# Hedgehog attention, a two-dimensional Fourier mix and an FFN on one core: a loop of batches against one woven order

## The chip, the cores and the metric

One core of a Trainium2 chip. The time is device microseconds of one execution; the table below gives the median of three runs of the kernel before.

## What is computed

For each of 8 batches, 8 heads, 576 positions and 64 channels per head, the attention maps queries and keys through 128 features and both signs, then mixes without a softmax; the result of all heads, 576 x 512 numbers, goes through a Fourier mix, a layer norm and an FFN with a hidden width of 2,048.

```python
def phi(x):
    proj = einsum('bhsd,df->bhsf', x, w_phi)
    proj = proj - max(abs(proj), axis=-1)
    return concatenate([exp(proj), exp(-proj)], axis=-1)
kv = einsum('bhsf,bhsd->bhfd', phi(k), v); z = sum(phi(k), axis=2)
x = (phi(q) @ kv) / (phi(q) @ z + 1e-06)          # heads side by side: 576 x 512
u = x + real(fft(fft(x, axis=1), axis=2))
un = (u - mean(u)) / sqrt(var(u) + 1e-06)          # per row
out = u + maximum(un @ w_ch1, 0) @ w_ch2
```

Inputs and outputs are float32; the kernels compute their matmuls in bf16.

## The kernel before

A batch goes through three functions. `attention_stage` loads queries, keys and values with 15 DMAs on POOL's queue, 128 positions each, which turn float32 to bf16 on the way, and turns queries and keys with ten DMA transposes on SP (L195, L196) into QT and KT, which have one buffer each. `attention_core` loops over the 8 heads. For each it projects the queries twice, once with features on the partitions (psqh, L210 and L214, for the exponentials QPhp and QPhn) and once with positions on the partitions (psqs, L225, only for the largest absolute value), and the keys once (pskk, L235). VectorE takes the maxima (L243, L246), ScalarE the exponentials (L220, L221, L260, L261), VectorE scales the values (L264, L268); then come the key-value products (L276), the products with the queries (psnum, L290 and L296), and the division on VectorE (L306 to L313) into X. 64 contraction rows per projection means half of the array's rows.

`fft_ffn` copies X to bf16 (XB, L325), takes column means with a matmul of ones (pmb) and column sums (pcs), and subtracts the means (XF). The DFT over positions is 80 matmuls of 288 columns (psD, L361; in every group of five the last has 64 rows); the one over channels is 40 of 512 columns (psu, L385 and L390). U is their sum with X. Row statistics are taken with VectorE, an inverse square root by shifts and Newton steps on small tiles (L416 to L443), the scaled rows on ScalarE (UN, L449), and TensorE transposes them (pUT, L456). The FFN is 128 matmuls of 288 columns with a relu on ScalarE per group of four (psh, L474 and L481) and 80 of 512 columns (pso, L486), whose sum with U is stored.

The cosine and sine tables are made at the start by `gen_dft` with VectorE and ScalarE, 36 sines over blocks of 288 or 256 columns. The two FFN weights load once. The outer loop stages batch b + 1, runs its `attention_core`, and then `fft_ffn` of batch b; a scheduler orders the instructions by what they depend on, with the DFT's front end at a high priority.

Of the kernel before, what the change touches and what calls it, by code (L numbers as in the profile page):

```python
# [10 lines left out]
AT = mybir.ActivationFunctionType  # L12
# [3 lines left out]
F32R = mybir.dt.float32r  # L16
BF16 = mybir.dt.bfloat16
I32 = mybir.dt.int32

BATCH_LIST = None  # L20
DEBUG_DUMP = False

MAGIC = 12582912.0


@with_exitstack
def kernel(
# [15 lines left out]
    NSC = 5  # L43
    NCC = C // 128
    NHH = HID // 128
    assert (B, H, S, D, DF, C, HID) == (8, 8, 576, 64, 128, 512, 2048)

    def msz(js):
        return 128 if js < 4 else 64

    batches = list(range(B)) if BATCH_LIST is None else list(BATCH_LIST)

    const = ctx.enter_context(tc.tile_pool(name="const", bufs=1))
    stage = ctx.enter_context(tc.tile_pool(name="stage", bufs=2))
    transp = ctx.enter_context(tc.tile_pool(name="transp", bufs=1))
    headp = ctx.enter_context(tc.tile_pool(name="headp", bufs=2))
    small = ctx.enter_context(tc.tile_pool(name="small", bufs=4))
    dwork = ctx.enter_context(tc.tile_pool(name="dwork", bufs=2))
    xpool = ctx.enter_context(tc.tile_pool(name="xpool", bufs=2))
    fpool = ctx.enter_context(tc.tile_pool(name="fpool", bufs=1))  # L60
    outp = ctx.enter_context(tc.tile_pool(name="outp", bufs=2))
    psumA = ctx.enter_context(tc.tile_pool(name="psumA", bufs=2, space=bass.MemoryType.PSUM))
    _psumB = [None]

    def get_psumB():
        if _psumB[0] is None:
            _psumB[0] = ctx.enter_context(tc.tile_pool(name="psumB", bufs=4, space=bass.MemoryType.PSUM))
        return _psumB[0]
# [3 lines left out]
    eps_ap = const.tile([128, 1], F32, name="eps_ap")  # L72
    nc.vector.memset(eps_ap[:], 1e-06)
    sc2 = const.tile([128, 2, NSC], F32, name="sc2")
    nc.vector.memset(sc2[:, 0, :], 2.0)
    nc.vector.memset(sc2[:, 1, :], -1.0)

    wphi2 = const.tile([128, DF], BF16, name="wphi2")
    nc.gpsimd.dma_start(out=wphi2[0:64, :], in_=w_phi[:, :])
    nc.gpsimd.dma_start(out=wphi2[64:128, :], in_=w_phi[:, :])  # L80

    W1b = const.tile([128, NCC, HID], BF16, name="W1b")
    W2b = const.tile([128, NHH, 512], BF16, name="W2b")

    _wloaded = []

    def load_ffn_weights():
        if _wloaded:
            return
        _wloaded.append(True)  # L90
# [3 lines left out]
    onesS_b = const.tile([128, 128], BF16, name="onesS_b")  # L94
    nc.vector.memset(onesS_b[:], 1.0 / S)
    ones2_b = const.tile([128, 2], BF16, name="ones2_b")
    nc.vector.memset(ones2_b[:], 1.0)
    ident_b = const.tile([128, 128], BF16, name="ident_b")
    make_identity(nc, ident_b[:])

    CS_r = const.tile([128, NSC, S], BF16, name="CS_r")
    SS_r = const.tile([128, NSC, S], BF16, name="SS_r")
    CD_r = const.tile([128, NCC, C], BF16, name="CD_r")
    SDn_r = const.tile([128, NCC, C], BF16, name="SDn_r")

    def gen_dft(gen, dst_cos, dst_sin, nchunks, N, sin_sign, rowk, pcol):
        half = N // 2
        last = None
        for j in range(nchunks):
            for hb in range(2):  # L110
                mm = gen.tile([128, half], F32, tag="mm", name="mm")
                nc.vector.tensor_scalar_mul(
                    out=mm[:], in0=rowk[:, half * hb: half * hb + half], scalar1=pcol[:, j: j + 1]
                )
                q1 = gen.tile([128, half], F32, tag="q1", name="q1")
                nc.vector.tensor_single_scalar(out=q1[:], in_=mm[:], scalar=1.0 / N, op=ALU.mult)
                kq = gen.tile([128, half], F32, tag="kq", name="kq")
                nc.vector.tensor_scalar(
                    out=kq[:], in0=q1[:], scalar1=MAGIC, scalar2=MAGIC,
                    op0=ALU.add, op1=ALU.subtract,  # L120
                )
                mr = gen.tile([128, half], F32, tag="mr", name="mr")
                nc.vector.scalar_tensor_tensor(
                    out=mr[:], in0=kq[:], scalar=-float(N), in1=mm[:],
                    op0=ALU.mult, op1=ALU.add,
                )
                last = nc.scalar.activation(
                    out=dst_sin[:, j, half * hb: half * hb + half], in_=mr[:],
                    func=AT.Sin, scale=sin_sign * 2.0 * np.pi / N * (1.0 - 1e-7),
                )  # L130
                kqc = gen.tile([128, half], F32, tag="kqc", name="kqc")
                nc.vector.tensor_scalar(
                    out=kqc[:], in0=q1[:], scalar1=0.25, scalar2=MAGIC,
                    op0=ALU.add, op1=ALU.add,
                )
                kqc2 = gen.tile([128, half], F32, tag="kqc2", name="kqc2")
                nc.vector.tensor_single_scalar(
                    out=kqc2[:], in_=kqc[:], scalar=MAGIC, op=ALU.subtract
                )
                mrc = gen.tile([128, half], F32, tag="mrc", name="mrc")  # L140
                nc.vector.scalar_tensor_tensor(
                    out=mrc[:], in0=kqc2[:], scalar=-float(N), in1=mm[:],
                    op0=ALU.mult, op1=ALU.add,
                )
                last = nc.scalar.activation(
                    out=dst_cos[:, j, half * hb: half * hb + half], in_=mrc[:],
                    func=AT.Sin, scale=2.0 * np.pi / N * (1.0 - 1e-7), bias=halfpi[:],
                )
        return last

    def generate_constants():
        with tc.tile_pool(name="genc", bufs=1) as genc, tc.tile_pool(
            name="gent", bufs=1
        ) as gen:
            rowk_i = genc.tile([128, 640], I32, name="rowk_i")
            nc.gpsimd.iota(rowk_i[:], pattern=[[1, 640]], base=0, channel_multiplier=0)
            rowk = rowk_i[:].bitcast(F32)
            nc.vector.tensor_copy(out=rowk, in_=rowk_i[:])
            pcol_i = genc.tile([128, 9], I32, name="pcol_i")
            nc.gpsimd.iota(pcol_i[:], pattern=[[128, 9]], base=0, channel_multiplier=1)  # L160
            pcol = pcol_i[:].bitcast(F32)
            nc.vector.tensor_copy(out=pcol, in_=pcol_i[:])
            gen_dft(gen, CS_r, SS_r, NSC, S, 1.0, rowk, pcol)
            last = gen_dft(gen, CD_r, SDn_r, NCC, C, -1.0, rowk, pcol)
        return last

    def attention_stage(b):
        QS = stage.tile([128, NSC, H * D], BF16, tag="QS", name="QS")
        KS = stage.tile([128, NSC, H * D], BF16, tag="KS", name="KS")
        VS = stage.tile([128, NSC, H, D + 1], BF16, tag="VS", name="VS")  # L170
        nc.vector.memset(QS[64:128, NSC - 1, :], 0.0)
        nc.vector.memset(KS[64:128, NSC - 1, :], 0.0)
        nc.gpsimd.memset(VS[64:128, NSC - 1, :, :], 0.0)  # L173
        nc.vector.memset(VS[:, 0:NSC - 1, :, D:D + 1], 1.0)
        nc.vector.memset(VS[0:64, NSC - 1, :, D:D + 1], 1.0)
        for j in range(NSC):
            rows = msz(j)
            s0 = 128 * j
            nc.gpsimd.dma_start(
                out=QS[0:rows, j, :].rearrange("p (h d) -> p h d", h=H),  # L180
                in_=q[b, :, s0:s0 + rows, :].rearrange("h p d -> p h d"),
            )
            nc.gpsimd.dma_start(
                out=KS[0:rows, j, :].rearrange("p (h d) -> p h d", h=H),
                in_=k[b, :, s0:s0 + rows, :].rearrange("h p d -> p h d"),
            )
            nc.gpsimd.dma_start(
                out=VS[0:rows, j, :, 0:D],
                in_=v[b, :, s0:s0 + rows, :].rearrange("h p d -> p h d"),
            )  # L190
        QT = transp.tile([128, H // 2, 128 * NSC], BF16, tag="QT", name="QT")
        KT = transp.tile([128, H // 2, 128 * NSC], BF16, tag="KT", name="KT")
        for j in range(NSC):
            s0 = 128 * j
            nc.sync.dma_start_transpose(out=QT[:, :, s0:s0 + 128], in_=QS[:, j, :])  # L195
            nc.sync.dma_start_transpose(out=KT[:, :, s0:s0 + 128], in_=KS[:, j, :])  # L196

        return (QS, KS, VS, QT, KT)

# [347 lines left out]
```

## Time and profile before

| | before |
|---|---|
| median of 3 runs | 892.1 us (885.8 to 893.01) |
| profiled execution, its span | 893.2 us |
| TensorE, weight loads, VectorE, ScalarE, GpSimd busy | 673.9, 391.1, 467.0, 420.9, 110.2 us |
| mean granted TensorE clock | 0.893 |
| bytes read and written in HBM | 36.77 and 9.44 MB |

The profile is one execution. A busy share of TensorE counts its pipelined matmuls from start to modelled end, so a full slice says that work was there, not that it went at the highest rate. The granted clock is given as a share of 2.4 GHz; 0.5 is 1.2 GHz.

### The profile page before, as it was taken

What the parts mean: (1) busy time and instruction counts of PE and PEld (TensorE: products, weight loads), DVE (VectorE), ACT (ScalarE), POOL (GpSimd) and SP (SyncE); (2) the same over time, 40 slices, a digit from 0 to 9 for tenths busy, and PEclk for the clock granted to TensorE, in tenths of its full rate; (3) what the DMA queues carried; (4) which work ended last, traced back from release to release, by engine and by line L of the source; (5) the groups of instructions that cost most, each with busy time, mean ns of one, the idle gap of its engine ahead of it and who ended that gap; (6) DMA issues with size and microseconds to landing.
All of it is one profiled execution on the core that took longest, in us unless ns stands there. A gap on an engine that the chain in (4) does not pass through costs nothing.

```text
span 893.2 us, 13139 instructions
## 1 busy us (share of the span) xinstructions
PE 673.9 (75%) x5000; PEld 391.1 (44%) x5032; DVE 467.0 (52%) x1366; ACT 420.9 (47%) x886; POOL 110.2 (12%) x140
## 2 busy tenths in 40 slices
PE   0112439795996699795996699787996799699887
PEld 0002324463454445363454445364544545364463
DVE  8575635851477316951477316960577237833411
ACT  2599434373255425373155425373256606470270
POOL 8710140014000320014000320010000000000000
PEclk9999999877996889877996889878996899689989
DMA  9992190029100980029100980019100310001001
GB/s 99 147 196 19 32 107 1 1 30 110 54 1 1 93 82 18 1 27 113 54 2 1 90 85 18 1 26 73 43 1 1 59 54 1 1 1 48 6 1 53
DMA packets 164094, 39.15 MB, mean 44 GB/s; under 512 B 156864, under 2 KB 158912, under 8 KB 164032
## 3 DMA queue, kind: packets, MB, share of 16 engines
q0 software_dynamic: 115264, 18.39, 31.2%
q1 hardware_dynamic: 48768, 19.94, 10.9%
q8 instruction: 39, 0.64, 0.3%
q14 instruction: 23, 0.19, 0.1%
HBM read 36.77 MB, written 9.44 MB: 52 GB/s over the span
## 4 chain that ended last, share of the span: by engine, by line
PE 64%; ACT 11%; DVE 8%; DMA 6%; SPq 6%; issue 2%; POOL 2%; DVEq 0%; ACTq 0%; POOLq 0%
PE pso L486 16%; PE psh L474 12%; PE psD L361 12%; PE psu L385 4%; PE psu L390 3%; DMA VS<-in_v_dram 3%; SPq L195 3%; PE pskk L276 3%; SPq L196 3%; DMA QT<-QS 3%; PE pskk L235 3%; PE psqs L225 2%; PE psqh L210 2%; DVE MM L246 2%; PE psnum L290 2%
## 5 line engine op out<-in xcount | busy, mean ns | idle before, releaser
L474 PE MATMUL psh<-UNT,W1b 128*128 128x288 bf16 x1024 | 161.8, 320 | 16.7 <-ACT HT L481 16.7
L486 PE MATMUL pso<-W2b,HT 128*128 128x512 bf16 (+1 forms) x624 | 140.8, 380 | 0.8
L474 PEld LDWEIGHTS <-W1b 128*128 128x128 bf16 x1024 | 107.4, 109 | 57.9 <-issue 19.7
L481 ACT ACTIVATE HT<-psh 128x288 bf16<-128x288 f32 x256 | 97.9, 415 | 52.2 <-PE psh L474 46.0
L491 DVE TENSOR_TENSOR OUT<-pso,U 128x512 f32<-128x512 f32 (+1 forms) x40 | 27.6, 690 | 169.7 <-PE pso L486 169.7
L368 ACT CAST DT<-psD 128x288 bf16<-128x288 f32 x64 | 24.9, 404 | 155.2 <-PE psD L361 154.9
L486 PEld LDWEIGHTS <-HT 128*128 128x128 bf16 (+1 forms) x640 | 63.5, 100 | 73.5 <-issue 3.4
L276 PE MATMUL pskk<-VSCp,KPp 128*128 128x65 bf16 x320 | 23.4, 210 | 73.1 <-DVE VSCp L264 50.7
L361 PEld LDWEIGHTS <-XF 128*128 128x128 bf16 (+1 forms) x640 | 52.5, 98 | 55.3 <-issue 29.8
L243 DVE TENSOR_REDUCE MM<-psqs 128x5 f32<-128x640 f32 x64 | 52.7, 824 | 38.9 <-PE psqs L225 37.3
L220 ACT ACTIVATE QPhp<-psqh 128x640 bf16<-128x640 f32 x64 | 45.0, 704 | 53.3 <-PE psqh L214 48.5
L260 ACT ACTIVATE KPp<-pskk 128x640 bf16<-128x640 f32 x64 | 45.0, 702 | 52.2 <-DVE MM L246 39.0
L235 PE MATMUL pskk<-wphi,KT 64*128 64x128 bf16 x320 | 36.1, 248 | 39.8 <-DMA KT<-KS 38.1
L361 PE MATMUL psD<-CS_r,XF 128*128 128x288 bf16 (+1 forms) x320 | 62.8, 299 | 0.0
L361 PE MATMUL psD<-SS_r,XF 128*128 128x288 bf16 (+1 forms) x320 | 60.9, 298 | 0.0
L210 PE MATMUL psqh<-QT,wphi 64*128 64x512 bf16 x64 | 31.0, 484 | 39.4 <-DMA QT<-QS 29.7
L225 PE MATMUL psqs<-wphi,QT 64*128 64x128 bf16 x320 | 37.0, 258 | 25.8 <-ACT QPhn L221 21.1
L306 DVE TENSOR_TENSOR tmpg<-psnum,EE 128x325 f32<-128x325 f32 x64 | 31.7, 495 | 47.0 <-PE psnum L296 47.0
L276 PEld LDWEIGHTS <-KPp 128*128 128x128 bf16 x320 | 18.0, 107 | 87.0 <-ACT KPn L261 48.8
L246 DVE TENSOR_REDUCE MM<-pskk 128x5 f32<-128x640 f32 x64 | 52.0, 812 | 4.1 <-PE pskk L235 2.7
L173 POOL MEMSET VS<- 64x520 bf16 x8 | 4.5, 558 | 390.0 <-DVE VSCn L268 389.9
L225 PEld LDWEIGHTS <-QT 64*128 64x128 bf16 x320 | 24.5, 112 | 53.9 <-issue 33.8
(98 smaller groups left out, 1120.8 us busy)
## 6 DMA issues: line engine op xcount, KB each, us to landing
out_dram<-OUT SPq DMA_DIRECT2D x32, 256.0 KB, 2.0
QS<-in_q_dram POOLq DMA_DIRECT2D x32, 128.0 KB, 4.8
KS<-in_k_dram POOLq DMA_DIRECT2D x32, 128.0 KB, 4.7
VS<-in_v_dram POOLq DMA_DIRECT2D x32, 128.0 KB, 5.7
W1b<-in_moe_w_ch_dram POOLq DMA_DIRECT2D x1, 2048.0 KB, 14.6
W2b<-in_moe_w_ch_dram POOLq DMA_DIRECT2D x1, 2048.0 KB, 23.8
out_dram<-OUT SPq DMA_DIRECT2D x8, 128.0 KB, 2.3
QT<-QS SPq DMA_TRANSPOSE x40, 3.8
```

Of the source, the lines that this page charges most:

```text
L210: nc.tensor.matmul(psqh[:, 0:512], lhsT=wphi2[rr, :], rhs=QT[rr, pr, 0:512], start=True, stop=True,)
L220: nc.scalar.activation(out=QPh_p[:], in_=psqh[:, 0:640], func=AT.Exp, scale=1.0)
L225: nc.tensor.matmul(psqs_v[:, jj, :], lhsT=QT[rr, pr, 128 * jj: 128 * jj + 128], rhs=wphi2[rr, :], start=True, stop=True,)
L235: nc.tensor.matmul(pskk_v[:, jj, :], lhsT=KT[rr, pr, 128 * jj: 128 * jj + 128], rhs=wphi2[rr, :], start=True, stop=True,)
L243: nc.vector.tensor_reduce(out=MM[:, 0, :], in_=psqs_v, axis=AX.X, op=ALU.max, apply_absolute_value=True)
L246: nc.vector.tensor_reduce(out=MM[:, 1, :], in_=pskk_v, axis=AX.X, op=ALU.max, apply_absolute_value=True)
L260: nc.scalar.activation(out=KPp[:], in_=pskk_v, func=AT.Exp, scale=1.0)
L276: nc.tensor.matmul(pskk[:, c0: c0 + D + 1], lhsT=KP[:, jj, :], rhs=VSC[:, jj, :], start=(jj == 0), stop=(jj == NSC - 1),)
L361: nc.tensor.matmul(psD[:, 0:288], lhsT=XF[0:M, js, 128 * cc: 128 * cc + 128], rhs=MAT[0:M, js, 288 * kb: 288 * kb + 288], start=(js == 0), ...
L474: nc.tensor.matmul(psh[:, 0:288], lhsT=W1b[:, cc, 128 * hh: 128 * hh + 128], rhs=UNT[:, cc, 288 * hf: 288 * hf + 288], start=(cc == 0), st ...
L481: nc.scalar.activation(out=out_ap, in_=psh[:, 0:288], func=AT.Relu)
L486: nc.tensor.matmul(pso[0:M, :], lhsT=HT[:, hh, 128 * kk: 128 * kk + M], rhs=W2b[:, hh, :], start=(hh == 0), stop=(hh == NHH - 1),)
```

## The change

The kernel is written anew around the same sums.

- The input is real, and only the real part of the transform is kept. The first DFT therefore works on folded channels (FEO: channel n plus or minus channel 512 - n, 256 each) and folded rows (row s plus or minus row 576 - s), with 320 table columns instead of 576, and the second one makes 320 rows; the other 256 are the same rows read backwards in channels (`pu[:, C-1:0:-1]`). So that mirrored rows stand on the same partition, queries are loaded in another order, in blocks of 16 with the exponentials' order reversed, and the output is stored in such blocks.
- Centring subtracts row 0 of X (`pm`, a matmul with one contraction row) instead of the column means.
- Projections are made for four or eight head blocks at once, in two banks, with the two halves of the contraction rows in turn; one exponential covers 1,024 columns.
- GpSimd scales the values, divides by the denominator, and folds the channels. The sum of the exponentials' scale over the values uses ScalarE for the factors.
- The factor 1/sqrt(var) is applied after the FFN, in the sum that forms the output; before it only the mean is subtracted (VectorE). GpSimd takes the power -0.5. The normalised rows are turned by DMA transposes on SP.
- 64 remaining rows of the second FFN product run on two halves of the array's columns.
- No scheduler orders the work: `weave` takes one step of a stream per letter of three strings. F is the FFN (68 steps), M attention's products and the mixing (23), T exponentials (18), P query maxima, R key maxima, S scaled values, N the norm, K, V, Q loads, A, B transposes, D row folds, W weights, C tables. A letter whose needs are not met is held and tried again. Before the first F, START has one whole batch and half of the next one's T; FIRST and PERIOD hold each step of a batch once (FIRST half of T more), PERIOD is repeated.

```diff
-        QT = transp.tile([128, H // 2, 128 * NSC], BF16, tag="QT", name="QT")
-        for j in range(NSC):
-            nc.sync.dma_start_transpose(out=QT[:, :, s0:s0 + 128], in_=QS[:, j, :])
...
+        def keys(pr):
+            psk = pj.tile([128, 2, 4, DF], F32, tag="pj", name="psk")
+            for x in range(4):
+                for jj in range(2):
+                    rr = slice(64 * jj, 64 * jj + 64)
+                    nc.tensor.matmul(
+                        psk[:, jj, x, :], lhsT=turned_k[b][0][rr, 4 * pr + x, :], rhs=wphi2[rr, :],
+                        start=True, stop=True,
+                    )
+            for sgn, KP in ((1.0, KPp), (-1.0, KPn)):
+                nc.scalar.activation(out=KP[...], in_=psk[:], func=AT.Exp, scale=sgn)
+                yield
...
+        def scale_v(pr):
+            for sgn, VC in ((1.0, VCn), (-1.0, VCp)):
+                nc.scalar.activation(out=VC[:, hs, :, D:D + 1], in_=MK[...], func=AT.Exp, scale=sgn)
+                eng = nc.vector if b == 0 and sgn < 0 else nc.gpsimd
+                eng.tensor_tensor(out=VC[:, hs, :, 0:D], in0=values[b][0][...], in1=VC[...], op=ALU.mult)
...
+        def fold(h):
+            for i, op in enumerate((ALU.add, ALU.subtract)):
+                eng = nc.vector if b == 0 and i else nc.gpsimd
+                eng.tensor_tensor(
+                    out=FEO[:, :, i, a:a + D], in0=X[:, :, a:a + D],
+                    in1=X[:, :, C - a:C - a - D:-1], op=op,
+                )
...
+            nc.gpsimd.tensor_tensor(
+                out=X[:, :, D * h:D * h + D], in0=cb[:, :, 0:D], in1=rd[:].to_broadcast([128, 5, D]), op=ALU.mult,
+            )
...
-                            psD[:, 0:288],
-                            lhsT=XF[0:M, js, 128 * cc: 128 * cc + 128],
-                            rhs=MAT[0:M, js, 288 * kb: 288 * kb + 288],
+        for i, mat, dst in ((1, SS, ET), (0, CS, DT)):
+            for mt in range(2):
+                for c in range(3):
+                    nc.tensor.matmul(
+                        ps[:, mt, 0:NK], lhsT=CEO[:, c, i, 128 * mt:128 * mt + 128],
+                        rhs=mat[:, c, :], start=(c == 0), stop=(c == 2),
+                    )
+            nc.scalar.copy(out=dst[:], in_=ps[:, :, 0:NK])
...
-                nc.scalar.activation(
-                    out=UN[0:M, kk, :], in_=U[0:M, kk, :], func=AT.Identity,
+            nc.vector.tensor_scalar(
+                out=UN[0:M, c, :], in0=X[0:M, c, 0:C], scalar1=mv[0:M, c, 0:1], op0=ALU.subtract,
+            )
+            nc.sync.dma_start_transpose(out=UT[:, :, 128 * c:128 * c + M], in_=UN[0:M, c, :])
...
+            nc.vector.scalar_tensor_tensor(
+                out=U[:, c, 0:C], in0=po[:], scalar=rs[:, c:c + 1], in1=U[:, c, 0:C],
+                op0=ALU.mult, op1=ALU.add,
+            )
+            store(b, U, c)
...
+    with tc.manual_schedule():
+        count()
+        load_first()
+        step("B")
+        step("A")
+        clear_pads()
+        weave(START + FIRST + PERIOD * (B - 1))
```

## Rows read from the trace of the kernel before

**Rows 1.** The page's busy time of each engine over the span.
```profile
PE 673.9 (75%) x5000; PEld 391.1 (44%) x5032; DVE 467.0 (52%) x1366; ACT 420.9 (47%) x886; POOL 110.2 (12%) x140
```
**Rows 2.** The page's 40 slices: busy tenths of TensorE, and its granted clock.
```profile
PE   0112439795996699795996699787996799699887
...
PEclk9999999877996889877996889878996899689989
```
**Rows 3.** The page's chain that ended last, by engine.
```profile
PE 64%; ACT 11%; DVE 8%; DMA 6%; SPq 6%; issue 2%; POOL 2%; DVEq 0%; ACTq 0%; POOLq 0%
```
**Rows 4.** The chain in order of time: start us, us, what.
```profile
185.60 4.61 PE psh L474 x22
...
319.97 10.74 PE pso L486 x49
...
420.45 10.74 PE pso L486 x49
...
871.70 10.74 PE pso L486 x49
```
**Rows 5.** Stretches of 10 us: busy us of PE, PEld, DVE, ACT, POOL; clock; DMA.
```profile
270.00:280.00 10.00, 3.50 (x32) 2.31 (x32) 9.05 (x50) 4.27 (x10) 0.00 (x0) 0.56 0.01 2
300.00:310.00 10.00, 4.01 (x29) 2.62 (x27) 0.66 (x3) 0.94 (x3) 2.54 (x4) 0.77 1.50 137
...
340.00:350.00 10.00, 10.00 (x86) 5.53 (x86) 6.45 (x19) 7.00 (x17) 0.00 (x0) 1.00 0.06 15
860.00:870.00 10.00, 10.00 (x84) 8.00 (x82) 0.00 (x0) 8.35 (x21) 0.00 (x0) 1.00 0.01 2
```
**Rows 6.** Waits (us in total, times, longest); one SP transpose of the timeline.
```profile
PE pskk L235 <- DMA KT<-KS: 38.1, 10, 17.4
...
302.39 1.35 SPq L195 DMA_TRANSPOSE QT<-QS  x1
```
**Rows 7.** Timeline of TensorE: start us, us, engine, line, operation.
```profile
17.40 0.28 PE L235 MATMUL pskk<-wphi,KT 64*128 64x128 bf16 x1 [17.40 <-DMA KT<-KS]
...
291.13 0.19 PE L290 MATMUL psnum<-kvh,QPhp 128*128 128x65 bf16 x1
...
291.41 0.19 PE L296 MATMUL psnum<-kvh,QPhn 128*128 128x65 bf16 x1
...
293.42 0.44 PE L235 MATMUL pskk<-wphi,KT 64*128 64x128 bf16 x5
...
827.45 1.71 PE L361 MATMUL psD<-CS_r,XF 128*128 128x288 bf16 x10
829.09 1.71 PE L361 MATMUL psD<-SS_r,XF 128*128 128x288 bf16 x10
```
**Rows 8.** ScalarE by line: count, then busy us, mean ns, idle before.
```profile
L481 ACT ACTIVATE HT<-psh 128x288 bf16<-128x288 f32 x256 | 97.9, 415 | 52.2 <-PE psh L474 46.0
...
L220 ACT ACTIVATE QPhp<-psqh 128x640 bf16<-128x640 f32 x64 | 45.0, 704 | 53.3 <-PE psqh L214 48.5 <-PE psnum L296 4.3 <-PE pUT L456 0.6
...
L284 ACT CAST kvh<-pskk 128x130 bf16<-128x130 f32 x64 | 17.5, 273 | 52.7 <-PE pskk L276 52.7
...
L145 ACT ACT_TABLE_LOAD x12 | 15.4, 1283 | 0.2
```
**Rows 9.** VectorE by line.
```profile
L243 DVE TENSOR_REDUCE MM<-psqs 128x5 f32<-128x640 f32 x64 | 52.7, 824 | 38.9 <-PE psqs L225 37.3
...
L306 DVE TENSOR_TENSOR tmpg<-psnum,EE 128x325 f32<-128x325 f32 x64 | 31.7, 495 | 47.0 <-PE psnum L296 47.0
...
L310 DVE RECIPROCAL rden<-comb 128x5 f32<-128x5 f32 x64 | 12.0, 187 | 1.2
```
**Rows 10.** GpSimd by line.
```profile
L179 POOL DMA_DIRECT2D QS<-in_q_dram x40 | 34.7, 869 | 82.8 <-DMA QT<-QS 43.6 <-DMA KT<-KS 30.6 <-DMA W1b<-in_moe_w_ch_dram 7.2
...
L173 POOL MEMSET VS<- 64x520 bf16 x8 | 4.5, 558 | 390.0 <-DVE VSCn L268 389.9
```
**Rows 11.** DMA issues: KB each, median us to landing.
```profile
W1b<-in_moe_w_ch_dram POOLq DMA_DIRECT2D x1, 2048.0 KB, 14.6
```

More of the change, by code (lines that the diff above doesn't have):

```diff
@@ new lines, in clear_pads, with load, make_k @@
+    def clear_pads():
+        nc.gpsimd.memset(QPHP[:, :, 576:640], 1.0)
+        nc.gpsimd.memset(QPHN[:, :, 576:640], 1.0)
+        for i in range(2):
+            nc.vector.memset(MQ[i][64:128, :, 4:5], 0.0)
+            nc.vector.memset(MV[i][64:128, 4, :], 1.0)
+    def load(pieces, which):
+        for i in which:
+            nc.gpsimd.dma_start(out=pieces[i][0], in_=pieces[i][1])
+    def make_k(b):
+        KS = stage.tile([128, H, 256], BF16, tag="KS", name="KS")
+        KS4 = stage.tile([64, H, D], BF16, tag="KS4", name="KS4")
+        pieces = [(KS4[:], k[b, :, 512:576, :].rearrange("h p d -> p h d"))]
+        for g in range(2):
+            hs = slice(4 * g, 4 * g + 4)
+            pieces.append(
+                (KS[:, hs, :], k[b, hs, 0:512, :].rearrange("h (p j) d -> p h (j d)", j=4))
+            )
+        return (KS, KS4), pieces
@@ new lines, in load_first, with turn_k @@
+    def load_first():
+        staged["k", 0], pk_ = make_k(0)
+        values[0], pv_ = make_v(0, 2)
+        staged[0], pq_ = make_q(0)
+        load(pk_, (0, 1, 2))
+        nc.gpsimd.memset(V4P[:], 0.0)
+        nc.gpsimd.memset(V4N[:], 0.0)
+        load(pv_, (2, 0, 1))
+        load(pq_, (0,))
+        load(pv_, (3,))
+        load(pq_, (1, 2, 3))
+        for name in "KVQ":
+            taken[name] = 1
+    def turn_k(KS, KS4):
+        KT = attn.tile([128, 16, 128], BF16, tag="KT", name="KT")
+        KT4 = attn.tile([128, 4, 64], BF16, tag="KT4", name="KT4")
+        nc.sync.dma_start_transpose(out=KT4[:], in_=KS4[:].rearrange("p h d -> p (h d)"))
+        for g in range(2):
+            nc.sync.dma_start_transpose(
+                out=KT[:, 8 * g:8 * g + 8, :],
+                in_=KS[:, 4 * g:4 * g + 4, :].rearrange("p h x -> p (h x)"),
+            )
+        return KT, KT4
@@ new lines, in heads @@
+        order = (4, 0, 7, 1, 6, 2, 5, 3) if b else range(H)
+        ready = {7: (0,), 6: (1,), 5: (2,), 3: (3,)} if b else {5: (3,), 6: (2,), 7: (1, 0)}
+        kvh = []
+        for h in range(H):
+            kvh.append(keyvalue(h))
+            yield
+        for h in order:
+            combine(h, kvh[h])
+            if h == 4:
+                nc.gpsimd.tensor_copy(out=X[:, :, C:C + 1], in_=X[:, :, 256:257])
+            for a in ready.get(h, ()):
+                fold(a)
+            yield
@@ new lines, in forward @@
+            store(b, U, c)
+            yield
+        po = pb.tile([128, C], F32, tag="pb", name="pso")
+        for hh in range(NHH):
+            g = 64 * (hh % 2)
+            nc.tensor.matmul(
+                po[g:g + 64, :], lhsT=HT[:, hh, 512:576], rhs=W2b[:, hh, :],
+                start=(hh < 2), stop=(hh >= NHH - 2),
+            )
+            if hh % 4 == 3 and hh < NHH - 1:
+                yield
+        for g in (0, 64):
+            nc.vector.scalar_tensor_tensor(
+                out=U[0:64, 4, 0:C], in0=po[g:g + 64, :], scalar=rs[0:64, 4:5],
+                in1=U[0:64, 4, 0:C], op0=ALU.mult, op1=ALU.add,
+            )
@@ new lines, in forward, with fetch_k, arrive_k, fetch_v @@
+        store(b, U, 4)
+        yield
+    staged, parts = {}, {}
+    def fetch_k(b):
+        staged["k", b], pieces = make_k(b)
+        load(pieces, range(3))
+        yield
+    def arrive_k(b):
+        turned_k[b] = turn_k(*staged.pop(("k", b)))
+        yield
+    def fetch_v(b):
+        values[b], pieces = make_v(b, 1)
+        load(pieces, range(3))
+        yield
+    def fetch_q(b):
+        staged[b], pieces = make_q(b)
+        load(pieces, range(4))
+        yield
+    def arrive(b):
+        turned_q[b] = turn_q(*staged.pop(b))
+        parts[b] = features(b)
+        yield
@@ new lines, in part, with run, fold_later @@
+    def part(i):
+        def run(b):
+            yield from parts[b][i]
+        return run
+    def fold_later(b):
+        yield from folds[b]
+    STREAMS = {
+        "F": (forward, 68), "M": (mixing, 23), "D": (fold_later, 2), "N": (normalise, 6),
+        "P": (part(0), 6), "T": (part(1), 18), "R": (part(2), 5), "S": (part(3), 5),
+        "K": (fetch_k, 1), "V": (fetch_v, 1), "Q": (fetch_q, 1), "A": (arrive, 1),
+        "B": (arrive_k, 1), "W": (load_ffn_weights, 2), "C": (constants, 7),
+    }
@@ new lines, in weave @@
+    def weave(plan):
+        held = []
+        for name in plan:
+            held = [x for x in held if not step(x)]
+            if name in held or not step(name):
+                held.append(name)
+        while any(taken[x] < STREAMS[x][1] * (1 if x in "WC" else B) for x in STREAMS):
+            assert any([step(x) and taken[x] < STREAMS[x][1] * B for x in STREAMS])
+    with tc.manual_schedule():
[5 more added lines that the diff above has]
+        weave(START + FIRST + PERIOD * (B - 1))
```

965 lines of the change are left out of this document (567 added, 398 removed).

## The prediction

> **What bounds the kernel now.** I read the page from the top. TensorE is busy 75% of the span, VectorE 52%, ScalarE 47%, GpSimd 12% [rows 1], so no engine is full on the whole; the slices show a first sixth with TensorE nearly empty and then a pattern that repeats [rows 2]. The chain that ended last lies 64% on TensorE, 11% on ScalarE, 8% on VectorE, 6% each on DMA and on SP's queue [rows 3]: it changes hands. The chain in order of time gives the two lengths that the sum needs [rows 4]. The first long stretch of FFN matmuls starts at 185.60; the second FFN product starts its long stretch at 319.97 for one batch and at 420.45 for the next, so a batch costs 100.5 us; the last one starts at 871.70. The profiled execution is the span of 893.2 us, 1.1 us over the median of the runs shown (892.1); I sum against 893.
>
> Inside a period, three stretches of 10 us tell why [rows 5]. At 340 TensorE is full at the full granted clock. At 270 (layer norm) VectorE is full, TensorE works 3.5 us, and the clock falls to 0.56, so to 1.2 GHz for most of it. At 300 nearly everything stands while DMA and POOL run: SP's transposes of the next batch's keys and queries have one buffer, and the key projections wait 38.1 us for KT in all, ten times [rows 6].
>
> **The prices,** at the full clock. 288 columns: 84 matmuls in 10 us, 0.119 each [rows 5]. 512 columns: 49 in 10.74, 0.219 [rows 4]. 65 columns: from 291.13 to 291.41 nine steps, 0.03 each [rows 7]. 128 columns on half the rows: five in 0.44, at most 0.088 each, and 0.04 if the 0.28 that one alone takes is its latency; I take 0.07 [rows 7]. The old DFT runs ten matmuls of 288 columns per 1.64 us, 0.165 each, where 0.119 is the price: in each group of five the last uses 64 rows, so going between whole and half array costs about 0.23 per group [rows 7]. By these a period of before holds, in us: FFN 128 x 0.119 = 15.2 and 80 x 0.219 = 17.5; DFT 80 x 0.165 = 13.2 and 40 x 0.219 = 8.8; projections 8 x 0.289 + 80 x 0.07 = 7.9; 160 small ones 4.8; means, sums and transposes 3.1. That is 70.5 of 100.5: 30 are waits and half clock.
>
> **The change, part by part.** *Folds.* Channel and row symmetry leave 12 matmuls of 320 columns for the first DFT (between 0.132, the FFN price scaled, and 0.183, the old one scaled; I take 0.15) where there were 80, 12 of 512 where there were 40, and 3 for one odd column: 1.8 + 2.6 + 0.5 = 4.9 instead of 22.0. *Centring* by an all-ones product over five chunks becomes one matmul on one row, 0.2; the column sums go; the 20 transposes on TensorE become 5 DMA transposes. *Projections* keep their 80 half-array matmuls (5.6) and 10 wide ones (8 x 0.219 + 2 x 0.11 = 2.0). *Small ones* stay: 4.8. *FFN:* 15.2, then 64 x 0.219 = 14.0 and 16 on half the columns at the same price, 3.5; two for turning the query maxima, 0.4. *Switching* between array shapes, some 12 groups beyond those in the 0.07 price, x 0.23 = 2.8. Sum: 4.9 + 0.2 + 5.6 + 2.0 + 4.8 + 15.2 + 14.0 + 3.5 + 0.4 + 2.8 = 53.4 us of TensorE per batch if half-array matmuls follow one another.
>
> They may not. The new order alternates the two halves of the rows into two banks. If pairs overlapped, the projections would fall by 3.8 and the 16 half-column ones by 1.7, to 48. No row shows a pair on two halves, only runs on one half. The Trainium skill, "TensorEngine Tiling (Array Packing)", Key Properties, says that tiles work in parallel but that a change of tiling mode drains the array; by its first half a batch would cost 48, by its second the 0.23 stays. The trace agrees with the second half only, at 0.23 per group [rows 7]. I take 50, the middle, and 3 us of waits that no weaving hides: a period of 53.
>
> *What lies beside it,* per batch, must stay under 53. ScalarE: its prices are 0.415 for 288 columns and 0.704 for 640 [rows 8], so 0.00082 per column more; 16 exponentials of 1,024 at 1.02, 4 of 512 at 0.60, 32 relus 13.3, DFT copies 1.4 + 0.4, two row copies 1.2, 22 small ones at most 0.273 [rows 8]: 40.9. VectorE [rows 9]: 0.824 for 640 and 0.495 for 325 columns give 0.00104 per column: 9 maxima of 1,024 at 1.22 and one of 512, 11.7; eight heads x (0.495 + 0.495 + 0.187) = 9.4; folds 1.7, centring 1.5, adding X 3.8, normalising 7.7, the last sums 4.1: 39.9. The scaling of the normalised rows leaves ScalarE because the factor moves behind the FFN into the sum that exists anyway. All this is cover only as long as each in-order queue gets its work in time; without it the excess of the fullest over TensorE is added.
>
> *GpSimd takes over* scaling the values, dividing by the denominator and the channel fold: 28 instructions, 4,096 + 1,024 + 2,560 + 2,560 = 10,240 elements per partition. Its own rows show a memset of 520 elements at 0.558 us, so 1.07 ns each [rows 10]; the same kind of work on VectorE costs 0.495 for 325, 1.52 ns [rows 9]. That is 11 to 16 us, with ten loads at 0.87 [rows 10] 20 to 25 of 53: costed at nothing. The price of a two-operand GpSimd instruction stands in no row, so nothing excludes more; it enters the path beyond 53. The Trainium skill, "GPSIMD Engine Reference", Engine selection, advises against just this, at about half VectorE's speed; from its section on elementwise cycles (2.6 at 1.2 GHz) I estimate 22 us, 31 with the loads, still below the period.
>
> *Queues.* SP now issues 11 transposes per batch (3 for K, 3 for Q, 5 for the normalised rows, up to 2 x 1.3 us for the wide ones by 1.35 each [rows 6]), about 19 us, and 12 stores; a store that waits for VectorE holds the next transposes. POOL's loads wait for the buffer that SP's transposes free, and queued behind them are the value scalings and divisions that combine and key-value products need. That is the place of the new waits. Loads read 512 B to 1 KB runs instead of 256 B; W1, in large pieces, landed 14.6 us after issue [rows 11], so a batch's 3.5 MB fit many times over.
>
> *Start.* Before, the first projection ran at 17.40 [rows 7] and the FFN at 185.60. The order written out gives the first batch its whole attention, mixing and norm and the second half its projections before any FFN step. I take 17 for the first keys again, then ScalarE as the fullest: 27.6 for batch 0 without relus, 10 for tables (5 absolute values, 10 sines, two table loads at 1.283; the 12 loads of before [rows 8] came from mixing sines and exponentials), 10 for half of batch 1: 65, and 1 for the tail of the norm: 66. Its bounds are 58 and 80.
>
> *Sum.* Counting letters in the three strings: 66 for the start; a first period with half a batch of projections extra, 55; five full periods, 5 x 53 = 265; one with the last batch's mixing but no projections, 45; one of FFN alone, 15.2 + 14.0 + 3.5 = 33; the last store 3. **467, say 465 us.**
>
> **Rivals.** *A, the forecast* (period 49 to 57, 430 to 505). For it: 30 of 100 us are waits, spread over different resources, and FFN matmuls of an earlier batch can fill them. *B, the queues hold each other:* a POOL load or SP store waits, behind it stands what TensorE wants, and the clock falls as at 270. If the three kinds of stall keep a third of their 30 us, a period is 63: 80 + 66 + 315 + 52 + 35 + 3 = 551. *C, pairs overlap and nothing waits:* 46 per period, 58 + 48 + 230 + 39 + 31 + 3 = 409. For it speaks the alternation, against it that DVE and ScalarE at 40 leave little slack. *D, slower:* GpSimd's elementwise becomes the bound. For 893 us the periods before the last FFN (6.9, counting the short ones by their share of 53) have to take (893 - 66 - 36) / 6.9, 115 us, so 106 beside the loads for 10,240 elements: from 10 ns each it decides. Rows show a tenth of that. At 13 ns a period is 142, the time about 1,080. *E, the weave does not weave:* steps whose needs are not met are held back until the parts run one after another, 70 to 100 per period, 600 to 890, little or no gain.
>
> **Chances.** A 0.58, C 0.16, B 0.17, E 0.05 (one in five of it within 1%), D 0.04. The range 415 to 540 holds A, the upper part of C and the lower part of B. Faster by over 1% (about what a measurement here can tell from no change) 0.95, within 1% 0.01, slower 0.04.
>
> **What would show it.** Right: F steps evenly spaced 50 to 55 us per batch from about 66 on; clock at 1.0 outside the start; psD and pu together near 5 us per batch; TensorE over 85% busy in a period. C shows as projection pairs at under 0.04 per matmul. B shows as POOL or SP waits before VC, X or UT. D shows as GpSimd busy over 90%. The number is wrong first where the start is not 66, then where the period is set by VectorE or GpSimd instead of TensorE.

## The result, and the profile after

The changed kernel takes 491.86 us, median of four runs (489.34 to 498.27), against 891.68 for the kernel before (a fourth execution beside the three above): a ratio of 0.5517, 95% interval 0.5489 to 0.5544. The forecast was 465, the range 415 to 540. The profiled execution has a span of 491.2 us; it is the one read here. Executions over 1.5% above the fastest of their kernel are left out of ratios and intervals, not of medians.

The page, to be read beside [rows 1 to 3]: busy time of each engine, TensorE's slices and clock, and the chain by engine.

```profile
PE 410.0 (83%) x3897; PEld 250.1 (51%) x3920; DVE 330.3 (67%) x620; ACT 301.3 (61%) x650; POOL 267.2 (54%) x345
...
PE   0257271879999899899998999989998999999995
...
PEclk9999996798999999899999999999998999999999
...
PE 50%; DVE 19%; DMA 16%; ACT 9%; POOL 3%; issue 2%; DVEq 0%; SPq 0%; POOLq 0%; ACTq 0%
```

TensorE lost 264 us of busy time, but 402 us went: the rest are waits and half clock. Behind the first fifth TensorE's slices are now nearly all 8 or more, where [rows 2] has holes. DMA's part of the chain rose from 6 to 16% while that of SP's queue fell from 6% to nothing, a first hint at what follows.

The last sums of a batch's FFN date the periods (timeline of VectorE; the end is start plus duration): batch 0, batch 5, batch 7.

```profile
147.80 1.52 DVE L747 SCALAR_TENSOR_TENSOR X<-pso,rs,X 64x512 f32<-64x512 f32 x2
...
410.36 1.53 DVE L747 SCALAR_TENSOR_TENSOR X<-pso,rs,X 64x512 f32<-64x512 f32 x2 [0.64 <-PE pso L740]
...
485.77 1.53 DVE L747 SCALAR_TENSOR_TENSOR X<-pso,rs,X 64x512 f32<-64x512 f32 x2 [1.10 <-PE pso L740]
```

The first FFN matmul ran at 87.26. So, against the terms of the sum:

| | forecast | measured |
|---|---|---|
| start, to the first FFN matmul | 66 | 87.3 |
| first period | 55 | 62.0 |
| five full periods | 265 | 262.6 (52.5 each) |
| mixing of the last batch, no projections | 45 | 42.5 |
| FFN alone | 33 | 32.9 |
| last store | 3 | 3.9 |

The five full periods are right to 1%; ahead of 149 the sum is 28 us short, and its later terms give 4 of them back. Four stretches of 10 us (columns as in [rows 5]): the end of the start at half clock, the first period, and two of full periods. The least busy stretches there, 200 to 210 and 260 to 270, still have 8.24 and 8.02 us of TensorE, at clocks of 0.83 and 0.94: nothing like those at 270 and 300 of [rows 5] is left.

```profile
80.00:90.00 10.00, 6.18 (x66) 4.44 (x67) 7.50 (x11) 5.80 (x15) 9.05 (x11) 0.50 0.84 80
100.00:110.00 10.00, 7.10 (x102) 5.60 (x102) 5.72 (x14) 6.45 (x15) 4.23 (x7) 1.00 1.02 134
210.00:220.00 10.00, 10.00 (x151) 8.12 (x151) 8.84 (x21) 6.00 (x16) 5.88 (x9) 1.00 1.66 114
240.00:250.00 10.00, 9.37 (x49) 3.70 (x50) 9.66 (x20) 8.43 (x14) 4.16 (x4) 1.00 0.52 92
```

### The profile page after: what moved, and what is told of

The parts are those of the page before. It is cut to its first block, busy times and chain, and to the rows that moved or that the text cites. A ratio compares the mean times of both kernels' runs of the same rounds, so it can differ in the third digit from the quotient of the medians.

```text
span 491.2 us, 10032 instructions
## 1 busy us (share of the span) xinstructions
PE 410.0 (83%) x3897; PEld 250.1 (51%) x3920; DVE 330.3 (67%) x620; ACT 301.3 (61%) x650; POOL 267.2 (54%) x345
## 4 chain that ended last, share of the span: by engine, by line
PE 50%; DVE 19%; DMA 16%; ACT 9%; POOL 3%; issue 2%; DVEq 0%; SPq 0%; POOLq 0%; ACTq 0%
PE pso L725 18%; PE psf L713 16%; DMA UT<-UN 8%; DMA QT<-QS 4%; PE psD L621 3%; DVE MK L375 3%; DVE UN L673 3%; ACT HT L718 2%; DMA out_dram<-X 2%; DVE st L671 2%; PE pso L740 2%; PE kv L544 2%; DVE cb L571 2%; POOL X L574 1%; ACT KPp L361 1%
## 5 line engine op out<-in xcount | busy, mean ns | idle before, releaser
L713 PE MATMUL psf<-UT,W1b 128*128 128x288 bf16 x1024 | 153.6, 295 | 8.7 <-DMA UT<-UN 7.4
L718 ACT ACTIVATE HT<-psf 128x288 bf16<-128x288 f32 x256 | 103.3, 413 | 81.8 <-PE psf L713 74.4
L725 PE MATMUL pso<-W2b,HT 128*128 128x512 bf16 x491 | 119.4, 380 | 2.9 <-issue 1.1
L574 POOL TENSOR_TENSOR X<-cb,rd 128x320 f32<-128x320 f32 x64 | 45.9, 722 | 62.1 <-DVE rd L573 61.6
L725 PEld LDWEIGHTS <-HT 128*128 128x128 bf16 x512 | 46.2, 98 | 59.7 <-issue 10.7
L330 POOL TENSOR_TENSOR VCn<-VS,VCn 128x512 bf16<-128x512 bf16 x32 | 34.5, 1079 | 51.3 <-ACT VCn L325 49.2
L507 POOL TENSOR_TENSOR FEO<-X 128x320 f32<-128x320 f32 x60 | 51.9, 885 | 2.4
L419 DVE TENSOR_REDUCE MQ<-psq 128x8 f32<-128x1024 f32 (+1 forms) x40 | 38.8, 1007 | 19.5 <-PE psq L411 19.4
L375 DVE TENSOR_REDUCE MK<-psk 128x8 f32<-128x1024 f32 x32 | 38.4, 1216 | 5.4 <-ACT KPp L361 5.3
L469 ACT ACTIVATE QPHN<-psh 128x1024 bf16<-128x1024 f32 x32 | 33.5, 1047 | 0.0
L330 POOL TENSOR_TENSOR VCp<-VS,VCp 128x512 bf16<-128x512 bf16 x28 | 30.3, 1084 | 0.0
```

The lines of the kernel that those rows point to most:

```text
L330: eng.tensor_tensor(out=VC[:, hs, :, 0:D], in0=values[b][0][:, hs, :].rearrange("p h (j d) -> p h j d", d=D), in1=VC[:, hs, :, D:D + 1].to ...
L375: nc.vector.tensor_reduce(out=MK[:, 2 * pr:2 * pr + 2, :].rearrange("p e (jp jj) -> p jj (e jp)", jj=2), in_=tiles[pr][:], axis=AX.X, op=A ...
L419: nc.vector.tensor_reduce(out=o, in_=i[:], axis=AX.X, op=ALU.max, apply_absolute_value=True)
L469: nc.scalar.activation(out=o, in_=psh[:], func=AT.Exp, scale=sgn)
L507: eng.tensor_tensor(out=FEO[:, :, i, a:a + D], in0=X[:, :, a:a + D], in1=X[:, :, C - a:C - a - D:-1], op=op,)
L574: nc.gpsimd.tensor_tensor(out=X[:, :, D * h:D * h + D], in0=cb[:, :, 0:D], in1=rd[:].to_broadcast([128, 5, D]), op=ALU.mult,)
```

## The experiments

All are edits of the changed kernel. Ratios are to the kernel before; the changed kernel's is 0.5517. A period is the mean of the five full ones in the profiled execution (52.5 in the changed kernel).

**Is a period TensorE's work?** First, two edits that leave nothing out. The keys' load moved away from the last norm transposes:

```diff
-PERIOD = "MKFMFMP...FTMQMFF..."
+PERIOD = "MFMFMP...FTMQKMFF..."
```

> The changed kernel with one letter moved: the next keys' load (three DMAs on POOL's queue) goes out behind the query load in the middle of a period, some 30 us earlier, not beside the last norm transposes. Theory (a period of 52 us is TensorE's work plus some 3 us of waits; the one wait left is that the last normalised rows need 10 us to land because key and value loads fill the DMA engines at that moment): landing in about 5 us, the 2 us gap of TensorE and the half clock behind it go, 2 to 3 us per period, 470 to 482 us against 492. Rival (the landing is late because of SP's queue or because the values load is enough to delay it, or TensorE has other work there): 487 to 495.

488.91 us, 0.5492 (0.5472 to 0.5512): not told apart from no change. The chain still shows the last norm transposes landing after 8 to 12 us; the values' load and the key transposes were still there. The theory, as far as it hung on the keys' load, failed.

Then the pairs on two halves of the array, taken apart:

```diff
-            for x in range(4):
-                for jj in range(2):
+            for jj in range(2):
+                for x in range(4):
...
-            g = 64 * (hh % 2)
+            g = 64 * (hh // 8)
```

> The changed kernel with the same matmuls in another order: four on one half of the rows, then four on the other (keys and query maxima), and the 16 FFN matmuls of the last rows eight on one half of the columns, then eight on the other. Theory (pairs on two halves overlap, and TensorE's work sets the period): the 80 small ones go from 0.041 to 0.06 to 0.08 each, the 16 from 0.116 to 0.219, so 3 to 5 us per batch, 515 to 530 us. Rival (TensorE has slack in a period, another engine sets it): at most 1 us per batch, 490 to 500.

490.88 us, 0.5507 (0.5464 to 0.5549), a period 51.9: no change. But the edit did not do what it was meant to. The timeline of TensorE, changed kernel and then this one, shows that the two halves still ran side by side:

```profile
249.20 1.92 PE L740 MATMUL pso<-W2b,HT 128*64 128x512 bf16 x16
251.91 0.30 PE L544 MATMUL kv<-VCp,KPp 128*128 128x65 bf16 x4
254.71 0.40 PE L411 MATMUL psq<-wphi,QT 64*128 64x128 bf16 x8 [0.63 <-DMA QT<-QS]
```
```profile
250.26 2.16 PE L740 MATMUL pso<-W2b,HT 128*64 128x512 bf16 x13
...
252.26 0.38 PE L740 MATMUL pso<-W2b,HT 128*64 128x512 bf16 x1
252.29 0.38 PE L643 MATMUL pu<-CD,DT 128*64 128x512 bf16 x1
...
253.03 0.24 PE L544 MATMUL kv<-VCp,KPp 128*128 128x65 bf16 x2
...
255.78 0.41 PE L411 MATMUL psq<-wphi,QT 64*128 64x128 bf16 x8
```

One behind the other, thirteen at the 0.219 of 512 columns would need 2.8 us; they took 2.16, and the last ones ran beside those of `pu`, which also use half the columns. From the first of the 16 to the next matmul of another kind it is 2.71 us in the changed kernel and 2.77 here. Eight on half the rows take 0.40 and 0.41. In all TensorE is busy 410.0 and 411.5 us.

So this run says nothing on whether a period is TensorE's work. The next expectation takes it for more TensorE work without more time; its theory L, a loop through the queues, has to stand on the runs that follow.

**Cutting the loop.** The norm transposes left out, the FFN reading a constant:

```diff
-            nc.sync.dma_start_transpose(out=UT[:, :, 128 * c:128 * c + M], in_=UN[0:M, c, :])
...
-        UT = unp.tile([128, NCC, S], BF16, tag="UT", name="UT")
+        UT = UTC[b % 2]
```

> The changed kernel without the five DMA transposes of the normalised rows: the FFN reads a constant. Theory L, formed because more TensorE work and an earlier key load moved nothing: a loop through the queues sets the 52 us, from one batch's FFN sum to the next's: sum (238.2 in the trace), SP's eight stores (5.2), three norm transposes (4.8), query transposes (to 254.7), query maxima, the last norm transposes (258.2, landed 268.5), the FFN's second half and its second product up to the sum (291.9). Without these transposes the loop is cut and TensorE's 46 to 49 us is left: 450 to 470 us. Theory P (TensorE's work plus 3 us of waits): only the 2 us gap and its half clock go, 472 to 482 us. Rival: another engine sets the period, 488 to 495.

475.7 us, 0.5352 (0.5323 to 0.5381). The last three full periods are 48.5, 48.6, 48.5 (the five are 49.2 on average), and TensorE has next to no gap: in the stretch below it is busy 51.88 of 52.00. So TensorE's work is 48.5 us per batch, and the norm transposes cost 4 us in these periods, 3.3 on the mean of five. The time lies in theory P's range (472 to 482) and misses theory L's: what limits a period without these transposes is shown, but not which theory is right.

```profile
202.00:254.00 52.00, 51.88 (x530) 31.64 (x529) 39.02 (x71) 37.60 (x83) 33.59 (x42) 0.98 0.63 80
```

**Less TensorE work.** Half of the first FFN product left out (`for cc in range(2)`).

> The changed kernel with half of the first FFN product left out (two of four contraction chunks: 64 matmuls, 7.6 us of TensorE per batch). Theory P (TensorE's work sets the period): 6 to 7.6 us per batch, 432 to 445 us. Theory L (the loop through sums, stores, transposes and the second half of the FFN): only what lies on the loop counts, 32 of them, 3 to 4 us per batch, 458 to 470 us. Rival (VectorE, ScalarE or GpSimd): no change, 485 to 493.

480.56 us, but the four runs spread from 471.27 to 488.89, so only this holds: 7.6 us less per batch, 61 in all, brought between 3 and 21. TensorE waits longer for the same thing: in the profiled execution, the longest of the four, 3.63, 3.71, 8.20 and 5.71 us in four of the periods, where the changed kernel has 1.54 to 2.26 (timeline):

```profile
209.71 1.62 PE L713 MATMUL psf<-UT,W1b 128*128 128x288 bf16 x6 [3.63 <-DMA UT<-UN]
```

That refutes "a period is TensorE's work"; theory L forecast more than came, 458 to 470.

**Less VectorE work.** Maxima over 64 of the 128 features (`in_=psk[..., 0:64]`); the other 64 are left out.

> The changed kernel with the maxima of keys and queries taken over the first 64 of 128 features: 10 VectorE instructions per batch half as wide, 5 us of VectorE per batch. Theory L (loop): two of them lie on the loop, 1 to 1.5 us per period, and 5 in the start, 472 to 482 us. Theory P (TensorE): only the start gains, 485 to 490. Rival V (VectorE's in-order queue sets the period): 4 to 5 us per period and the start, 445 to 460.

479.73 us, 0.5393 (0.5356 to 0.543), a period 50.9: in theory L's range, not in the others'. The first FFN matmul came 4.0 us earlier, batch 0's FFN ended 7.7 earlier, five periods brought 8. So VectorE's share shows in the start first; in a period 5 us less of it are worth 1.6.

**Rearranging SP's queue.** Three versions that compute everything. Eight stores issued at the end of the FFN:

```diff
-            store(b, U, c)
+            if c != 1:
+                store(b, U, c)
...
         store(b, U, 4)
+        store(b, U, 1)
```

> The changed kernel with the eight block stores of the first two row groups issued at the end of a batch's FFN instead of behind the second sum, so that on SP's queue the next batch's norm and query transposes go ahead of them; nothing is left out. Theory L: the loop loses up to 5.2 us of SP and the wait behind it, until TensorE's work is the bound, so 2 to 5 us per period, 458 to 480 us. Theory P: under 1 us per period, 486 to 494. Rival: the stores then hold the last norm transposes or the key transposes, slower by some us per period, 495 to 520.

522.19 us, 0.5878 (0.5843 to 0.5912), a period 56.9: slower than even the rival's range. The stores now stand before the last norm transposes, which miss their time; TensorE then waits 5.91. SP's queue, and TensorE:

```profile
266.39 7.79 SPq L695 DMA_DIRECT2D out_dram<-X  x8
274.28 1.22 SPq L677 DMA_TRANSPOSE UT<-UN  x1
...
280.32 2.10 PE L713 MATMUL psf<-UT,W1b 128*128 128x288 bf16 x8 [5.91 <-DMA UT<-UN]
```

Key load and key transposes earlier (the letters K and B moved behind D and Q):

> The changed kernel with two letters of each period moved: the keys' load goes out once their buffer is free, and the key transposes behind the query load in the middle of the period, when SP's queue is idle, so that only the values' load shares the DMA engines with the last norm transposes. Nothing is left out. Theory L (a loop through SP's queue and the landing of the last norm transposes sets the 52.5 us; without norm transposes a period was 48.5): the landing falls from 10 to about 5 us, 3 to 4 us less per period for five periods, 470 to 480 us. Rival 1 (the values' load or the row count is enough to make it late): 487 to 494. Rival 2 (the key transposes, issued earlier, now stand before the eight stores and the norm transposes): 494 to 510.

507.25 us, 0.571 (0.5685 to 0.5735), a period 55.4: rival 2. The wait before the FFN's second half is gone, but the key transposes queue between the stores and the norm and query transposes, and the query maxima wait 1.00 to 3.91, here 2.36:

```profile
304.23 5.14 SPq L695 DMA_DIRECT2D out_dram<-X  x8
309.48 1.20 SPq L273 DMA_TRANSPOSE KT<-KS  x1
310.80 2.71 SPq L275 DMA_TRANSPOSE KT<-KS  x2
313.60 3.90 SPq L677 DMA_TRANSPOSE UT<-UN  x3
...
323.08 0.61 PE L411 MATMUL psq<-wphi,QT 64*128 64x128 bf16 x8 [2.36 <-DMA QT<-QS]
```

A second buffer for the turned keys, so that they may be turned before the stores (the letters K and B move too, and small scratch tiles make room):

```diff
+        KT = attn.tile([128, 16, 128], BF16, tag="KT", name="KT", bufs=2)
-        "B": lambda b, i, n: n("K", b) >= 1 and n("T", b - 1) >= 9,
+        "B": lambda b, i, n: n("K", b) >= 1 and n("T", b - 1) >= 1 and n("T", b - 2) >= 9,
```

> The changed kernel with a second buffer for the turned keys, so that the key load can go out at 272 and the key transposes at about 280 of a period that has its sum at 292, while SP's queue is idle; small scratch tiles move into another tile to make room. Nothing is left out. It takes the key load and the key transposes from beside the last norm transposes, as the run before did, but without putting the key transposes between the sum's stores and the norm transposes, where they cost that run 3 to 4 us per period. Theory L: the last norm transposes land in about 5 us, TensorE has no gap before the FFN's second half, a period is 48.5 to 50 instead of 52.5 for five periods: 474 to 483 us. Rival 1 (the values' load alone keeps the landing at 10 us, or the loop waits elsewhere): 487 to 494. Rival 2 (the query load and the key transposes now collide and the query transposes come late): 494 to 505.

498.29 us, 0.5599 (0.5572 to 0.5625), a period 53.7 (57.1 the first of the five, 50.9 to 54.3 the others): rival 2. The second half of the FFN waits for nothing, but the key transposes still ran only at 239 to 245, just ahead of the stores, and the query transposes came late:

```profile
241.41 4.01 SPq L276 DMA_TRANSPOSE KT<-KS  x2
245.53 6.26 SPq L696 DMA_DIRECT2D out_dram<-X  x8
251.88 3.86 SPq L678 DMA_TRANSPOSE UT<-UN  x3
...
262.84 0.40 PE L412 MATMUL psq<-wphi,QT 64*128 64x128 bf16 x8 [3.53 <-DMA QT<-QS]
```

Theory L forecast a gain for all three orders, and none came.

**What the weave is worth.** The 68 FFN letters of FIRST and PERIOD moved behind the others.

> The changed kernel with the same steps, but the 68 FFN steps of each period behind all the others instead of spread among them. Theory (the weave is worth the overlap of TensorE's FFN with what VectorE, ScalarE and GpSimd do for later batches): a period becomes the 33 us of FFN plus 35 to 45 us in which VectorE works at 40 us per batch, 70 to 80, in all 590 to 660 us. Rival (folds and fewer instructions made the gain and the order matters little, since each engine's queue runs ahead on its own): under 530 us.

655.92 us, 0.7378 (0.7355 to 0.7401), a period 75.0. Two stretches of one period: first the other steps, at a clock of 0.69 with VectorE busy 31 of 40, then the FFN with VectorE nearly idle.

```profile
250.00:290.00 40.00, 22.67 (x261) 13.64 (x258) 31.12 (x58) 22.02 (x44) 27.17 (x34) 0.69 0.31 45
290.00:325.00 35.00, 34.29 (x236) 20.98 (x235) 7.11 (x12) 15.43 (x36) 6.19 (x8) 0.96 0.58 85
```

With the same steps and the FFN last, the gain over the kernel before is 233 us; spreading the FFN letters brings 164 more. What the folds and the other parts bring singly was not taken apart.

**GpSimd's elementwise work on VectorE** (`nc.gpsimd.tensor_tensor` to `nc.vector.tensor_tensor` in scaling, division and folds).

> The changed kernel with GpSimd's elementwise work (scaling of values, division, channel folds) on VectorE. Theory (GpSimd was free cover): VectorE gets 8 x 0.69 + 4 x 0.42 + 8 x 0.49 + 8 x 0.49, about 15 us per batch on top of its 41, less some 2 us because its own two-operand folds no longer lose time beside GpSimd; that passes the 52 us period, so 54 to 60 per period and a longer start, 515 to 560 us. Rival (the two engines get in each other's way so much that VectorE alone, with twice GpSimd's speed per element, is as good): 480 to 495 us.

540.4 us, 0.6084 (0.6057 to 0.6111), a period 57.6, VectorE busy 48.56 of 56.50 in the stretch below and the start 12 us longer. The theory's ranges hold, though VectorE is not full there.

```profile
230.00:286.50 56.50, 50.49 (x476) 29.08 (x473) 48.56 (x93) 35.33 (x76) 8.62 (x13) 0.97 0.68 78
```

**The start.** Batch 0's norm and twelve FFN steps ahead of batch 1's key maxima (the end of START `MNNRTTSQRMNNSTRTS` became `MNNMNNFFRTFFTSFFQRFFSTFFRTFFS`, and FIRST lost its first twelve F):

> The changed kernel with the end of the start in another order: the last norm steps of batch 0 go ahead of batch 1's key maxima and values, and twelve FFN steps are put among the latter instead of behind them. Nothing is left out. Theory (the start of 87 us ends on VectorE's in-order queue, where batch 1's maxima stand before batch 0's norm, and on TensorE's, where batch 1's projections wait for them): the first FFN matmul at 79 to 82 instead of 87, and 3 to 6 us off the whole, 485 to 489 us. Rival (the FFN steps taken out of the first period are missed there, and what was put off returns): the first matmul earlier, the time 490 to 495.

493.76 us, 0.5542 (0.5519 to 0.5565): no gain. In the profiled execution, of 503.39 us, the first FFN matmul ran at 80.81 instead of 87.26, behind a wait of 8.28 for the norm transposes, but batch 0's FFN ended at 153.4 instead of 149.3: the rival. The tables left out:

> The changed kernel without the cosine and sine tables: 15 VectorE passes, 5 absolute values, 10 sines and their two table loads are left out, and the tables hold a constant. The prediction's sum for the start (ScalarE is the fullest there and its work adds up; the tables are 10 us of it): 10 us less, 480 to 484 us. Theory S (after the last exponential at 45 us the start is a chain on VectorE through division, folds, mixing and norm, 42 us long; the sines lie beside it, the 15 passes delay only the first key maxima): 3 to 6 us less, 485 to 489 us.

489.61 us, 0.5496 (0.5466 to 0.5525); the first FFN matmul at 85.14, 2.1 earlier. The prediction's 10 us for tables are refuted; theory S is nearer, though even its 3 to 6 were too much.

## Why the prediction was right, and where it was not

**The start was mis-sized: 66 forecast, 87.3 measured, outside its bounds of 58 and 80.** The step that failed is "then ScalarE as the fullest ... and 1 for the tail of the norm". Keys at 17 and 27.6 of ScalarE make 44.6, and the last exponential of batch 0 did end at 44.7, but that is luck: the first key projections ran at 9.98 and 15.35, and from 17 to 44.75 ScalarE was busy 20.7 us and waited the rest, mostly for the keys' maxima (4.8). The fullest engine of the start is VectorE, 61.5 of 87.3 us against ScalarE's 45.6 (windows). And what follows stands behind the exponentials as a chain. Its waits from there, in order of time (start us, us, what):

```profile
43.83 0.92 ACT QPHN L469
...
44.96 0.51 DVE tg L566
...
57.98 1.52 DVE FEO L507 x2
...
64.92 2.85 PE psD L621 x10
...
71.25 0.69 DVE X L648
...
84.00 1.12 DVE MK L375
...
87.45 1.92 PE psf L713 x8
```

Eight divisions and the folds take 15 us, the mixing 12, five norms mixed with batch 1's maxima 16, and in these VectorE is busy 15.62 of 16.01. START holds all five maxima and value scalings of batch 1, not only half of its exponentials. Most of the 20 us that the sum had for tables and batch 1 lies beside this chain; with no cover to fill, an engine's sum is no bound for one batch's dependencies. Leaving the tables out moved the first FFN matmul by 2.1, halving the maxima by 4.0.

**The first period: 55 forecast, 62.0 measured.** It begins at half clock, and TensorE is busy 7.10 of ten at 100. That an earlier FFN start brought nothing suggests that this stretch waits for batch 1, not for the end of the start; with half the maxima it was 58, so VectorE counts here too. Which of its waits decides was not taken apart.

**A period: 53 forecast, 52.5 measured, by the right parts with one wrong name, and in part by luck.** TensorE's work was put at 50 between 53.4 and 48; without the norm transposes it is 48.5, so 1.5 too much work made up for 1 too little of waits. Of the prices, the first DFT was within its bounds (12 matmuls in 1.63, 0.136 each), the half-row ones were 0.041, the lower bound, not 0.07, and pairs on halves of the columns overlap, 0.12 each. The 2.8 us for switching between array shapes, 12 groups at 0.23, show nowhere in the timeline: eight half-row matmuls start at 256.94 and the next group at 257.27. The sum with these prices is about 46.5; where the other 2 us lie was not looked for. The Trainium skill, "TensorEngine Tiling (Array Packing)", Key Properties, says that different tiles work in parallel; the half-column pairs agree, 1.92 for 16 that would need 3.5 at 0.219 each.

The "3 us of waits that no weaving hides" are 4, and they are not scattered. They fit a loop from one batch's sum to the next's. The chain of the changed kernel, SP's queue in the first part of it, and the wait on TensorE:

```profile
238.20 0.76 DVE X L731
...
258.20 10.29 DMA UT<-UN
268.54 2.93 PE psf L713 x12
...
291.90 0.76 DVE X L731
```
```profile
239.01 5.15 SPq L695 DMA_DIRECT2D out_dram<-X  x8
244.26 4.81 SPq L677 DMA_TRANSPOSE UT<-UN  x3
...
249.95 1.58 SPq L285 DMA_TRANSPOSE QT<-QS  x1
...
258.20 2.07 SPq L677 DMA_TRANSPOSE UT<-UN  x1
```
```profile
268.54 2.93 PE L713 MATMUL psf<-UT,W1b 128*128 128x288 bf16 x12 [1.98 <-DMA UT<-UN]
```

291.90 - 238.20 = 53.7, that period. SP's queue carries the stores, the norm transposes and the query transposes one behind the other, 19.2 us from the first store to the last norm transpose with only one gap over 0.2 us (1.0, for VectorE); that transpose, whose input was ready at 254.85, takes 10.3 us to land; then the FFN's second half and second product follow on TensorE, 23.4. The prediction had put the new waits on SP and POOL and priced them in rival B only; its sum gave the stores no time, and they hold SP for 7.2 us of this period.

What speaks for the loop: cut, 48.5 and a full TensorE; 7.6 us less TensorE work per batch, 3 to 21 us in all instead of 61; three new orders on SP, each longer, each with TensorE waiting for a transpose. What is not shown is that a shorter loop pays: no order tried here was faster than 491.86 beyond the noise, and stores from another queue were not tried. Why the last norm transposes take 10 us is open too: with the keys' load moved away it was still 8 to 12. The loop also shows how a chain's share misleads: norm transposes hold 8.1% of it, 40 us, and leaving them out gave 16.

**GpSimd as cover was right, its price was not.** 11 to 16 us were taken from a memset and from VectorE; by line (busy us, mean ns) it is (51.9 + 45.9 + 34.5 + 30.3 + 12.6 + 10.0) / 8 = 23.2 per batch, so 31 with the loads, still under the period:

```profile
L507 POOL TENSOR_TENSOR FEO<-X 128x320 f32<-128x320 f32 x60 | 51.9, 885 | 2.4
L574 POOL TENSOR_TENSOR X<-cb,rd 128x320 f32<-128x320 f32 x64 | 45.9, 722 | 62.1 <-DVE rd L573 61.6
L330 POOL TENSOR_TENSOR VCn<-VS,VCn 128x512 bf16<-128x512 bf16 x32 | 34.5, 1079 | 51.3 <-ACT VCn L325 49.2 <-issue 2.0
```

The Trainium skill, "GPSIMD Engine Reference", Elementwise, had given 22 by the estimate in the prediction: the trace agrees with 23.2. The same page of the Trainium skill, Engine selection, gives such work to VectorE; done so, this kernel took 49 us longer, 540.4 against 491.86, with VectorE busy 48.56 of 56.50.

**The rivals.** B (queues hold each other) happened in kind but at 4 us per period. Of C the pairs came, but not the absence of waits. D and E did not happen: GpSimd is busy 54%, and the weave is worth 164 us. Of the signs, the clock was not at 1.0 outside the start, but at 0.97 in the stretch from 254 to 307.

## What to carry to other kernels

Sum an engine's work only where other batches fill its gaps; for the first batch add up its dependency chain, engine by engine. When a woven period stands a few us above its fullest engine, look for the loop that returns to itself one period later and for the in-order queue that it goes through; here, moving a letter on that queue moved the wait. Work given to a slower engine cost little while that engine stayed under the period. Before the time of an edit is read, its trace has to show that the edit did what it was meant to: the reordered matmuls ran side by side as before.

## What the runs showed of the hardware that was not expected

Matmuls on two halves of the array overlap even where the program puts eight on one half ahead of eight on the other: 16 of 512 columns start within 2.43 us then, and within 1.54 where the halves alternate; one behind the other at 0.219 it would be 3.3.

VectorE's own instructions with two operands in SBUF lose time beside GpSimd's: a row fold of 384 columns took 1,174 ns in the changed kernel, where GpSimd is folding at the time, and 551 ns where VectorE does GpSimd's share (VectorE by line, one row of each kernel). One that starts at 280.31 ends at 281.49, behind a fold of GpSimd's that ends at 281.07.

```profile
L520 DVE TENSOR_TENSOR SE<-FEO 128x384 f32<-128x384 f32 x7 | 8.2, 1174 | 0.0
```
```profile
L520 DVE TENSOR_TENSOR SE<-FEO 128x384 f32<-128x384 f32 x7 | 3.9, 551 | 0.0
```

With less work between longer waits TensorE also ran at a lower clock. The same 53 us, in the changed kernel and with half of the first FFN product left out, have a granted clock of 0.97 and 0.94:

```profile
254.00:307.00 53.00, 49.42 (x478) 29.73 (x479) 38.38 (x69) 35.73 (x79) 33.38 (x42) 0.97 0.76 87
```
```profile
254.00:307.00 53.00, 45.85 (x446) 24.96 (x442) 40.37 (x73) 35.98 (x82) 33.72 (x43) 0.94 0.76 92
```

So part of what that edit saved came back as matmuls at 1.2 GHz; with one profile of each, and that of the edit its longest execution, how much is not settled.
